# Unsplit weights for the first two subs, fp16 pairs in the second product, and an order by due times, in a chunked delta-rule attention with a gated product

## The chip, the cores and the metric

One core of a Trainium2 chip. The metric is the device time of one launch in microseconds.

## The reference, cut to what matters

A delta-rule recurrence over 768 steps for 4 x 8 heads of 48 features, then a gated product over its 3072 x 384 outputs. All inputs are float32 but the three weights, which are 64-bit floats.

```
for t in range(S):                       # q, k_n, v: [4, 8, 768, 48]
    y[:, :, t] = einsum('bhd,bhde->bhe', q[:, :, t], state)
    v_old = einsum('bhde,bhd->bhe', state, kt)
    state = state + bt * einsum('bhd,bhe->bhde', kt, vt - v_old)
x = y.transpose(0, 2, 1, 3).reshape(3072, 384)
out = ((x @ w_a) * (x @ w_b)) @ w_out    # w_a, w_b: 384 x 1536, w_out: 1536 x 384
```

## The kernel before

The 768 steps are cut into 24 chunks of 32, and two chunks (256 tokens over the batch) are a sub: 12 subs. The hidden dimension of 1536 is cut into 12 blocks of 128 (`NFC`). One block for one sub is called a unit here; there are 144.

Attention works in groups of chunks (`GROUPS`): two, five times four, two. `prep(g)` takes key norms and the key-key and key-query products of each chunk on TensorE (32 small matmuls, fp32, 64 columns wide) and, for the group, one power-of-two scale from a norm of queries and values. `solve(g)` inverts the 32 x 32 triangles of a group on VectorE, row by row; its instructions cover four chunks, and for the first group half of them is padding. `HALVES` has the first group's triangles solved in halves of 16, which small matmuls join (`wp`, `xp`). `steps(g)` goes through the chunks one after another: copy of the state (`sh`), state read `ks`, solve product `up`, output product `yp` (two groups of 32 small matmuls), state update into `S_ps`, then the scaled copy `y32`, a transpose, and the output as an fp16 high and low half (`xt`).

The gated product of a unit (`moe`): 18 matmuls of the first product, fp16, 256 columns wide (two factors, three slices of the model dimension, high x high, high x low and low x high). ScalarE copies one factor out (`a`), VectorE multiplies (`g`), ScalarE and VectorE make a high and a low half in fp32r (`ghl`). Two units later (`LAG`) `moe_out` does the second product: 6 matmuls, 384 wide, with `wo` in the same form, accumulated in two banks over the blocks of the sub.

A weight block arrives as 64-bit floats (1.15 MB). `weights` (line 550) builds the float32 bits with three integer operations on VectorE, takes the norm of the block (square on ScalarE, a matmul with ones), scales by a power of two, and splits it into halves in `wh` and `wo`; for the first four blocks (`LOWS`) the low halves come from fp32 matmuls with scaled identities. Since only three blocks have room while they arrive, the first two subs are done in pieces of two to four blocks, with partial sums in `acc`.

All operations are first written into a list (`Plan`), and `order` (line 391) sets the order on all engines: it simulates the engines with priced durations, forward and backward, six times over. `pack` keeps TensorE's small matmuls apart with a store of instruction words, and while TensorE has nothing in the first 80 us of the plan, `issue` (line 430) puts in filler matmuls of fp32 ones, 256 columns wide. Each engine, and SyncE's DMA issues, then run strictly in the written order. In the profile all planned operations have line 439, fillers line 430. An fp32 matmul shows as two records.

Of the kernel before, what the change touches and what calls it, by code (L numbers as in the profile page):

```python
# [28 lines left out]
GROUPS = [[0, 1]] + [list(range(i, i + 4)) for i in range(2, 22, 4)] + [[22, 23]]  # L29
# [3 lines left out]
HALVES = [1, 0, 0, 0, 0, 0, 0]  # L33

PARTS = [[i] for i in range(12)]
BOOST = {"first": 9e4, "prep0": 9e4, "solve0": 9e4, "steps0": 9e4, "w0": 7e4, "prep1": 5e4, "solve1": 5e4, "w1": 5e4, "w2": 4e4, "steps1": 5e4, "w3": 3e4, "w4": 3e4, "w5": 3e4, "w6": 3e4, "w7": 3e4, "w8": 3e4, "w9": 3e4, "w10": 3e4, "w11": 3e4}
LOWS = 4
# [3 lines left out]
URGENCY = {"first": 5000, "prep0": 5000, "solve0": 5000, "steps0": 5000, "w0": 3000, "w1": 2500, "w": 1500, "prep1": 3000, "solve1": 3000, "steps1": 3000, "prep": 200, "solve": 600, "steps": 500, "moe": 800, "moe_pe": 300}  # L41


class Op:
    __slots__ = ("eng", "calls", "dur", "move", "rd", "wr", "deps", "pri", "at", "end", "tag", "stream", "banks", "cold", "use", "words")

    def __init__(self, eng):
        self.eng, self.calls, self.dur, self.move = eng, [], 0.0, 0.0
        self.cold, self.use, self.words = 0.0, 0.0, 0
        self.rd, self.wr, self.deps, self.tag, self.banks = {}, {}, set(), "", set()  # L50


class Plan:
# [6 lines left out]
    def __init__(self, nc):  # L60
# [3 lines left out]
        self.stream = "first"  # L64
        self.masks = {}
# [115 lines left out]
    def add(self, eng, fn, name, args, kw):  # L181
# [5 lines left out]
        else:  # L187
            op = Op(eng)
            kind = self.stream + ("_pe" if self.stream == "moe" and eng == "PE" else "")
            op.pri = len(self.ops) - URGENCY.get(kind, URGENCY.get(kind.rstrip("0123456789"), 0))  # L190
# [12 lines left out]
        else:  # L203
            dur = self.price(eng, name, outs, ins, kw)
            op.dur += dur
            if eng == "PE":
                op.use += dur
                op.words += 4 if ins[0].dtype == F32 else 2
                if min(ins[0].shape[0], ins[0].shape[-1]) <= 64:
                    if len(op.calls) == 1:  # L210
                        op.dur += self.SWITCH
# [42 lines left out]

    def pack(self, pri, back=False):
# [10 lines left out]
        words, seen = self.STORE, 0.0  # L266
# [6 lines left out]
        while len(done) < n:  # L273
# [23 lines left out]
            while can[e] and i is None:  # L297
                i = heapq.heappop(can[e])[1]
                if ops[i].words and not back:
                    words, seen = min(self.STORE, words + (t - seen) * self.FETCH), t  # L300
                    if words < ops[i].words:
# [89 lines left out]
    def order(self):  # L391
# [23 lines left out]
        for o, o.at, o.end in zip(ops, best[1], best[2]):  # L415
            pass
# [697 lines left out]
```

## Time and profile before

| | us |
|---|---|
| runs | 685.86, 689.03, 690.97 (median 689.03) |
| profiled execution, first to last instruction | 692.9 |
| TensorE busy | 655.4 |
| VectorE busy | 418.9 |
| ScalarE busy | 256.8 |

The profiled execution's time is given by its span alone; it is 0.56% over the median of the runs. Busy time of TensorE includes the fillers, and a matmul's record lasts longer than the interval to the next one, since matmuls are pipelined.

### The profile page before, as it was taken

What the parts mean: (1) busy time and instruction counts of PE and PEld (TensorE: products, weight loads), DVE (VectorE), ACT (ScalarE), POOL (GpSimd) and SP (SyncE); (2) the same over time, 40 slices, a digit from 0 to 9 for tenths busy, and PEclk for the clock granted to TensorE, in tenths of its full rate; (3) what the DMA queues carried; (4) which work ended last, traced back from release to release, by engine and by line L of the source; (5) the groups of instructions that cost most, each with busy time, mean ns of one, the idle gap of its engine ahead of it and who ended that gap; (6) DMA issues with size and microseconds to landing.
All of it is one profiled execution on the core that took longest, in us unless ns stands there. A gap on an engine that the chain in (4) does not pass through costs nothing.

```text
span 692.9 us, 28147 instructions
## 1 busy us (share of the span) xinstructions
PE 655.4 (95%) x12994; PEld 557.3 (80%) x12994; DVE 418.9 (60%) x1125; ACT 256.8 (37%) x564; POOL 21.7 (3%) x28
## 2 busy tenths in 40 slices
PE   8879977999999989999999998999999999999997
PEld 6658755888888777788888886888877888878887
DVE  6686955888999797532436953336952249732222
ACT  2252434654822344443422244422243222332322
POOL 0000000000100010110000001100000000000000
PEclk9899985999999998999999998999999999999999
DMA  9522146441200031212200004000000000000000
GB/s 291 224 95 79 70 128 203 135 150 69 77 27 22 7 119 53 75 48 84 79 3 24 1 4 124 26 3 25 1 4 26 4 3 24 1 27 1 10 15 23
DMA packets 10581, 41.31 MB, mean 60 GB/s; under 512 B 1184, under 2 KB 4512, under 8 KB 7584
## 3 DMA queue, kind: packets, MB, share of 16 engines
q1 hardware_dynamic: 10464, 39.52, 17.3%
q8 instruction: 101, 1.65, 1.0%
q14 instruction: 16, 0.13, 0.1%
HBM read 34.80 MB, written 4.72 MB: 57 GB/s over the span
## 4 chain that ended last, share of the span: by engine, by line
PE 91%; issue 4%; DVE 4%; ACT 1%; DVEq 0%; ACTq 0%
PE bank L439 83%; PE bank L430 4%; PE S_ps L439 3%; DVE b L439 1%; DVE tmp L439 1%; DVE late L439 1%; ACT tt L439 0%; ACT sqf L439 0%; ACT late L439 0%; ACT u L439 0%; DVE xb L439 0%; DVE yt L439 0%; DVE f L439 0%; ACT wo L439 0%; DVE sw L439 0%
## 5 line engine op out<-in xcount | busy, mean ns | idle before, releaser
L439 PEld LDWEIGHTS <-wh 128*128 128x128 f16 x2592 | 242.8, 99 | 51.8 <-issue 21.0
L439 PE MATMUL bank<-xb,wh 128*128 128x256 f16 x1944 | 236.1, 275 | 0.0
L439 PE MATMUL bank<-wo,ghl 128*128 128x384 f32 x864 | 189.3, 353 | 0.0
L439 PEld LDWEIGHTS bank<-wo,ghl 128*128 128x128 f32 x864 | 144.5, 190 | 3.3
L439 ACT COPY a<-bank 128x256 f32<-128x256 f32 x144 | 53.5, 373 | 237.1 <-PE bank L439 236.8
L439 DVE TENSOR_TENSOR g<-bank,a 128x256 f32<-128x256 f32 x144 | 60.6, 421 | 126.7 <-ACT a L439 125.7
L439 DVE TENSOR_TENSOR ghl<-g,ghl 128x256 fp32r<-128x256 f32 x144 | 61.7, 430 | 33.6 <-ACT ghl L439 33.0
L439 PE MATMUL bank<-late,wh 128*128 128x256 f16 x648 | 80.2, 278 | 0.9 <-ACT late L439 0.4
L439 ACT CAST ghl<-g 128x256 fp32r<-128x256 f32 x144 | 58.1, 404 | 55.0 <-DVE g L439 54.4
L439 DVE TENSOR_TENSOR b<-b,tmp 128x60 f32<-128x60 f32 (+19 forms) x201 | 67.6, 336 | 4.4
L439 DVE TENSOR_TENSOR tmp<-b,b 128x60 f32<-128x60 f32 (+19 forms) x201 | 67.4, 335 | 4.5
L430 PE MATMUL bank<-ones 128*128 128x256 f32 x166 | 46.2, 427 | 3.3 <-DVE ones L439 3.3
L439 PEld LDWEIGHTS bank<-sh,rawb 48*32 48x32 f32 x2432 | 30.4, 110 | 16.0 <-issue 12.6
L439 PE MATMUL bank<-sh,rawb 48*32 48x48 f32 x2432 | 36.5, 209 | 6.4 <-issue 6.3
L430 PEld LDWEIGHTS bank<-ones 128*128 128x128 f32 x166 | 33.6, 212 | 8.7 <-DVE ones L439 3.2
L439 DVE STREAM_TRANSPOSE yt<-y 128x384 f32<-128x384 f32 x24 | 13.9, 577 | 33.5 <-ACT y L439 33.5
L439 PEld LDWEIGHTS bank<-f,tt 32*32 32x32 f32 x1472 | 19.5, 113 | 12.1 <-issue 7.7
L439 PE MATMUL bank<-u,at 32*32 32x48 f32 x1536 | 23.2, 206 | 5.5 <-issue 5.5
L439 PE MATMUL bank<-f,tt 32*32 32x48 f32 x1472 | 23.2, 214 | 5.1 <-issue 5.1
L439 PE MATMUL bank<-rawb 48*32 48x64 f32 x1280 | 22.6, 223 | 4.5 <-issue 4.5
L439 PEld LDWEIGHTS bank<-rawb 48*32 48x32 f32 x1280 | 19.9, 111 | 8.1 <-issue 7.8
L439 PEld LDWEIGHTS bank<-u,at 32*32 32x32 f32 x1536 | 19.1, 107 | 8.1 <-issue 6.2
(95 smaller groups left out, 490.3 us busy)
## 6 DMA issues: line engine op xcount, KB each, us to landing
rawb<-in_kqt SPq DMA_DIRECT2D x10, 896.0 KB, 6.0
late<-in_w SPq DMA_DIRECT2D x7, 1152.0 KB, 5.1
wh<-in_w SPq DMA_DIRECT2D x5, 1152.0 KB, 9.0
vnb<-in_vn SPq DMA_DIRECT2D x12, 384.0 KB, 3.2
out<-late SPq DMA_DIRECT2D x24, 192.0 KB, 1.9
knb<-in_kn SPq DMA_DIRECT2D x10, 384.0 KB, 3.4
late<-in_kqt SPq DMA_DIRECT2D x2, 896.0 KB, 5.9
late<-in_kn SPq DMA_DIRECT2D x2, 384.0 KB, 3.2
```

Source lines behind the costliest of these rows:

```text
L430: self.nc.tensor.matmul(self.pool[-1][:, 0:256], self.idle, self.idle.unsqueeze(1).broadcast_to([P, 2, P]), start=True, stop=True, skip_gr ...
L439: fn(*(self.place(a, lease) for a in args), **{k: self.place(a, lease) for k, a in kw.items()})
```

## The change

All groups have four chunks, the first ones too. The first two subs (`FULL`) use the float32 weights as `decode` makes them, with no norm and no split, in fp32 matmuls, and their outputs stay float32; block after block, without partial sums. The decoded blocks lie in one tile `wt`; when the second sub is through with a block, `split` writes the halves of the next one over it. `scales` takes the norms of all blocks for each factor, with the squares in bf16 as stationary operand and a column of ones. The second product's halves are fp16 instead of fp32r, with power-of-two scales for each factor and block (`gs`), for each chunk and batch (`n4`, from four squares and a matmul with `sel`), and for all of `w_out` (`big`). The order comes from one forward pass: each TensorE operation carries a due time, written by `slot` and `when`, the others take the latest time from what follows them. `stall` prices TensorE's instruction store in blocks of 256 words, and `pack` takes another ready operation where it would halt for over 250 ns. Key-query groups of the second group on, and the third and fourth chunk's joins, stand behind chunk 1's output product (`hold`). Fillers are 512 columns wide and end at 60 us of the plan.

```diff
-GROUPS = [[0, 1]] + [list(range(i, i + 4)) for i in range(2, 22, 4)] + [[22, 23]]
+GROUPS = [list(range(i, i + 4)) for i in range(0, NCH, 4)]
...
-EARLY = [(0, "k"), (0, "r"), (0, "b"), (2, "k"), (4, "k"), (2, "r"), (4, "r"), (0, "v"), (0, "w"), (1, "w"), (2, "v"), (4, "v"), (2, "w")]
+HALVES = [1, 0, 0, 0, 0, 0]
...
+FULL = 2
...
+LEADS = 4.0
+BASE, FRESH, UNIT = 46e3, 4.6e3, 3.75e3
+
+
+def when(v):
+    n = NFC * FULL
+    return BASE + (v * FRESH if v < n else n * FRESH + (v - n) * UNIT)
+
+
+def finish(c):
+    return 6 * c - 6 - (-2.5 if c == 4 else min(LEADS, 0.5 * max(0, c - 5)))
+
+
+def slot(c, piece):
+    if c < 2:
+        v = {
+            0: {"W": -10, "X": -9, "U": -8, "S": -7, "Q": -4, "A": -3.9},
+            1: {"W": -6.9, "K": -6, "X": -5.9, "U": -5, "Q": -4.5, "A": -4, "S": 0.2},
+        }[c].get(piece, -30)
+    elif c < 4:
+        v = (c - 2) * 5 + {"W": 0.5, "X": 1, "K": 1.5, "U": 2.5, "S": 3.5, "Q": 4, "A": 4.5}.get(piece, -30)
+    elif piece == "G":
+        v = 0.3 + 1.2 * (c - 4) if c < 8 else 18.5 + 1.2 * (c - 8) if c < 12 else finish(c - 6) - 0.5
+    else:
+        v = finish(c) - {"W": 7, "X": 6.5, "K": 5.5, "U": 4.5, "S": 3.5, "Q": 2.5, "A": 1.5}[piece]
+    return when(v)
...
+EARLY = [(0, "k"), (2, "k"), (0, "r"), (2, "r"), (0, "b"), (0, "v"), (0, "w"), (2, "v"), (1, "w"), (2, "w")]
...
+    def stall(self, o, t, pos, edge, come):
+
+        halt, each = 0.0, o.dur / o.words
+        end = pos + o.words
+        while end > edge:
+            enter = t + halt + (edge - pos) * each
+            if come > enter:
+                halt, enter = halt + come - enter, come
+            else:
+                enter = max(t, enter - self.AHEAD * each, come)
+            edge, come = edge + self.BLOCK, enter + self.FETCH
+        return halt, end, edge, come
...
+                if e == "PE" and not back and can[e] and self.stall(ops[i], t, pos, edge, come)[0] > self.STALL:
+                    other = [x for x in heapq.nsmallest(12, can[e]) if not ops[x[1]].banks - set(held)]
+                    other = [x for x in other if self.stall(ops[x[1]], t, pos, edge, come)[0] < 50.0]
+                    if other:
+                        can[e].remove(other[0])
+                        can[e].append((pri[i], i))
+                        heapq.heapify(can[e])
+                        i = other[0][1]
...
-    FETCH = 0.064
-    IDLE, SINCE, UNTIL = 440.0, 1500.0, 80e3
-    STORE = 512.0
-    SWITCH = 180.0
+    BLOCK, EDGE, FETCH, AHEAD, STALL = 256, 193, 3500.0, 30, 250.0
+    IDLE, SINCE, UNTIL = 870.0, 1500.0, 60e3
+    SWITCH = 108.0
...
-    PASSES = 6
...
+        pri = [0.0] * len(ops)
+        for i in range(len(ops) - 1, -1, -1):
+            o = ops[i]
+            late = [pri[k] - ops[k].dur - gap for k, gap in self.succ[i]]
+            pri[i] = min(late + [o.due] * (o.eng == "PE" or not late))
+            if o.stream == "load":
+                pri[i] = i - 1e9
+        for i, o in enumerate(ops):
+            if o.banks and o.eng != "PE":
+                pri[i] = min([pri[i]] + [pri[k] + self.SOON for k in o.deps if ops[k].eng == "PE"])
+        at, stop, done, total, (self.bind, self.fill) = self.pack(pri)
...
-    ghr = ring(cst, "ghl", LAG + 1, [P, 2, 256], F32R)
+    ghr = ring(cst, "ghl", LAG + 1, [P, 2, 256], F16)
...
+    WD = 6 * P + DM
+    wt = one("wt", [P, (NFC + 1) * WD], I32)
+    late = one("late", [P, 2816], I32)
+    stage = one("stage", [P, 4 * WD], I32)
...
+    slots = [late[:, 0 : 2 * WD]] + [stage[:, i * 2 * WD : (i + 1) * 2 * WD] for i in range(2)]
...
+    def decode(b):
+        load(b, "w")
+        st, d = slots[b % 3].rearrange("p (a l) -> p l a", l=2), wt[:, plain(b) : plain(b) + WD]
+        lo, hi = st[:, 0], st[:, 1]
+        V.tensor_scalar(d, hi, 5, 2, op0=ALU.logical_shift_left, op1=ALU.logical_shift_right)
+        V.scalar_tensor_tensor(d, hi, -0x40000000, d, op0=ALU.bitwise_and, op1=ALU.bitwise_or)
+        V.scalar_tensor_tensor(d, lo, 29, d, op0=ALU.logical_shift_right, op1=ALU.bitwise_or)
+        whole.add(b)
+        yield
+
...
+    def scales():
+        for b in range(NFC):
+            v = wf[:, plain(b) : plain(b) + 6 * P]
+            sq = sqr()
+            plan.due = when(b + 2.5)
+            A.activation(sq, v, AF.Square)
+            t = att()
+            with plan.group():
+                for m in range(2):
+                    for j in range(3):
+                        o = (3 * m + j) * P
+                        T.matmul(
+                            t[:, m : m + 1],
+                            sq[:, o : o + P],
+                            one16[:, 0:1],
+                            start=(m == j == 0),
+                            stop=(j == 2),
+                            skip_group_check=True,
+                        )
+            A.copy(norm[:, 2 * b : 2 * b + 2], t[:, 0:2])
...
+    def split():
+        for b in range(NFC):
+            v = wf[:, plain(b) : plain(b) + WD]
...
+            for m in range(2):
+                r, z = slice(3 * m * P, 3 * (m + 1) * P), zw[:, 2 * b + m : 2 * b + m + 1]
+                A.activation(h[:, 0, r], v[:, r], AF.Copy, scale=z)
+                V.scalar_tensor_tensor(h[:, 1, r], v[:, r], z, h[:, 0, r], op0=ALU.mult, op1=ALU.subtract)
+            e = eo[:, b : b + 1]
+            A.activation(o[:, 0], v[:, 6 * P :], AF.Copy, scale=e)
+            V.scalar_tensor_tensor(o[:, 1], v[:, 6 * P :], e, o[:, 0], op0=ALU.mult, op1=ALU.subtract)
...
+            if c // 2 < FULL:
+                if c % 2 == 0:
+                    xsub[c // 2] = xts[c // 2 % 4].rearrange("p (c j n) -> p c j n", c=2, j=3)
+                A.copy(yo, yi)
+                V.transpose(xsub[c // 2][:, c % 2].rearrange("p j n -> p (j n)"), y32)
+                yield
+                continue
...
+            for b in range(4):
+                A.activation(sqy, yb[:, b], AF.Square, accum_out=n[:, b : b + 1])
+            T.matmul(yp[:, 384:388], sel[:, 0:P], n, start=True, stop=True, skip_group_check=True)
+            V.tensor_scalar_max(t4, yp[:, 384:388], 2.0**-100)
+            root(e, t4)
+            flip(z, e, 13)
+            V.tensor_mul(yo, yi, z.unsqueeze(2).unsqueeze(3).broadcast_to([P, 4, 3, 32]))
+            V.tensor_mul(t4, e, sel[:, P : P + 4])
+            V.tensor_reduce(n[:, 0:1], t4, AX.X, ALU.add)
+            V.tensor_scalar(fact[:, c : c + 1], n[:, 0:1], n[:, 0:1], big[:, 3:4], op0=ALU.mult, op1=ALU.mult)
...
+                plan.due = when(NFC * s + fc + 0.33 * m)
+                if s < FULL:
+                    with plan.group():
+                        for j in range(3):
+                            o = plain(fc) + (m * 3 + j) * P
+                            T.matmul(
+                                ab[:, m, :].rearrange("p (c n) -> p c n", c=2),
+                                wf[:, o : o + P],
+                                xt[:, :, j, :],
+                                start=(j == 0),
+                                stop=(j == 2),
+                            )
+                    continue
...
-            A.copy(asb, ab[:, 0, :])
+            if s < FULL:
+                A.copy(asb, ab[:, 0, :])
+            else:
+                A.activation(asb, ab[:, 0, :], AF.Copy, scale=gs[:, fc : fc + 1])
             g32 = gr()
             V.tensor_mul(g32, ab[:, 1, :], asb)
-            ghl = ghr()
-            A.copy(ghl[:, 0], g32)
-            V.tensor_sub(ghl[:, 1], g32, ghl[:, 0].bitcast(F32))
+            if s < FULL:
+                ghl = g32
+            else:
+                ghl = ghr()
+                A.copy(ghl[:, 0], g32)
+                V.tensor_sub(ghl[:, 1], g32, ghl[:, 0])
...
+            plan.due = when(NFC * s + fc + LAG + 0.6 + 0.2 * i)
+            r = slice(i * P, (i + 1) * P)
+            if s < FULL:
+                o = plain(fc) + 6 * P
+                T.matmul(ops[s][i], ghl[:, r], wf[:, o : o + DM], start=first, stop=last)
...
-                part = acc[c] if s < 2 else None
-                final = fc == NFC - 1
-                ob = obs[c % 2] if final else part
-                if part is not None and c in started:
-                    V.scalar_tensor_tensor(ob, ops[s][i], facs[c], part, op0=ALU.mult, op1=ALU.add)
+                if s < FULL:
+                    A.copy(obs[i], ops[s][i])
                 else:
-                    A.activation(ob, ops[s][i], AF.Copy, scale=facs[c])
-                    started.add(c)
-                if final:
-                    SP.dma_start(out[c], ob)
-
-    started = set()
+                    A.activation(obs[i], ops[s][i], AF.Copy, scale=fact[:, c : c + 1])
+                SP.dma_start(out[c], obs[i])
...
+    queue.extend((s, list(range(NFC))) for s in range(2))
+    for b in range(3, NFC):
+        run_all(ws[b])
+        next(moes)
+        next(rest, None)
+    run_all(rest)
+    load(0, "m")
+    run_all(sc)
+    merge((moes, 8), (pr[1], 6))
+    merge((moes, 7), (sv[1], 8))
+    while pend:
+        moe_out(*pend.pop(0))
+    run_all(sp)
+    for g in range(1, NG):
```

## Rows read from the trace of the kernel before

**Rows 1.** The page: busy time, GB/s in 40 slices, two costly groups.

```profile
PE 655.4 (95%) x12994; PEld 557.3 (80%) x12994; DVE 418.9 (60%) x1125; ACT 256.8 (37%) x564; POOL 21.7 (3%) x28
...
GB/s 291 224 95 79 70 128 203 135 150 69 77 27 22 7 119 53 75 48 84 79 3 24 1 4 124 26 3 25 1 4 26 4 3 24 1 27 1 10 15 23
...
L439 PEld LDWEIGHTS bank<-wo,ghl 128*128 128x128 f32 x864 | 144.5, 190 | 3.3
...
L439 DVE STREAM_TRANSPOSE yt<-y 128x384 f32<-128x384 f32 x24 | 13.9, 577 | 33.5 <-ACT y L439 33.5
```

**Rows 2.** Stages: length, PE, PEld, DVE, ACT, POOL busy (instructions), clock, DMA.

```profile
46.00:122.00 76.00, 64.95 (x1388) 49.49 (x1388) 55.00 (x148) 29.41 (x56) 0.95 (x1) 0.83 0.34 110
122.00:259.00 137.00, 131.92 (x2508) 116.30 (x2509) 120.30 (x317) 64.71 (x141) 7.85 (x9) 1.00 0.23 75
259.00:433.00 174.00, 167.62 (x3757) 142.07 (x3749) 90.55 (x250) 66.47 (x149) 9.03 (x10) 0.96 0.17 51
```

**Rows 3.** Stages of TensorE's instructions that read the filler's ones.

```profile
0.00:122.00 122.00, 49.28 (x186) 0.86 0.46 155
```

**Rows 4.** Stages of TensorE's instructions that read the sub's input.

```profile
0.00:122.00 122.00, 4.43 (x36) 0.86 0.46 155
```

**Rows 5.** Timeline of TensorE late, product alone: start, length, instructions, count.

```profile
643.37 1.30 PE L439 MATMUL bank<-wo,ghl 128*128 128x384 f32 x6
644.52 2.14 PE L439 MATMUL bank<-xb,wh 128*128 128x256 f16 x18
646.41 1.30 PE L439 MATMUL bank<-wo,ghl 128*128 128x384 f32 x6
```

**Rows 6.** Timeline of TensorE where attention stands between products, two stretches.

```profile
363.79 1.30 PE L439 MATMUL bank<-wo,ghl 128*128 128x384 f32 x6
365.03 1.10 PE L439 MATMUL bank<-rawb 48*32 48x64 f32 x64
366.06 2.14 PE L439 MATMUL bank<-xb,wh 128*128 128x256 f16 x18
...
543.14 0.89 PE L439 MATMUL bank<-sh,rawb 48*32 48x48 f32 x64
...
544.77 1.16 PE L439 MATMUL bank<-xb,wh 128*128 128x256 f16 x9
```

**Rows 7.** TensorE's waits from 122 to 689.3 us: total, times, longest.

```profile
PE bank L439 <- issue: 11.2, 11, 2.6
```

**Rows 8.** Timeline of VectorE in the head.

```profile
27.35 1.01 DVE L439 STREAM_TRANSPOSE xn<-b 128x512 f32<-128x512 f32 x1
```

**Rows 9.** Timeline of TensorE in the head; brackets: idle before it.

```profile
30.88 0.74 PE L439 MATMUL bank<-b,tt 32*32 32x16 f32 x64
...
39.14 0.89 PE L439 MATMUL bank<-sh,rawb 48*32 48x48 f32 x64
...
47.78 1.35 PE L439 MATMUL bank<-f,tt 32*32 32x48 f32 x57 [2.11 <-issue]
...
58.22 0.88 PE L439 MATMUL bank<-u,at 32*32 32x48 f32 x64
...
61.68 2.13 PE L439 MATMUL bank<-xb,wh 128*128 128x256 f16 x18
```

**Rows 10.** The same timeline: fillers alone.

```profile
63.64 10.09 PE L430 MATMUL bank<-ones 128*128 128x256 f32 x46
```

**Rows 11.** What reads or writes the weight tile: durations min/median/max in ns.

```profile
L439 PEld LDWEIGHTS <-wh x2592: 95/98/181, 61.5 to 685.8; 128*128 128x128 f16 x200
L439 PE MATMUL bank<-xb,wh x1944: 269/273/421, 61.7 to 649.4; 128*128 128x256 f16 x195
...
L439 DVE SCALAR_TENSOR_TENSOR late<-wh,late x10: 1343/1352/1361, 69.5 to 125.9; 128x1152 int32<-128x1152 int32 x10
L439 PE MATMUL bank<-wh,neg x8: 323/326/527, 53.8 to 118.8; 128*128 128x384 f16 x8
...
DMA to landing us min/median/max: 5.4/9.0/18.7
```

More of the change, by code (lines that the diff above doesn't have):

```diff
@@ L39 @@
+EARLY = [(0, "k"), (2, "k"), (0, "r"), (2, "r"), (0, "b"), (0, "v"), (0, "w"), (2, "v"), (1, "w"), (2, "w")]
 LAG = 2
 LEAD = 4
[L41 removed]
 class Op:
[L45 removed]
+    __slots__ = ("eng", "calls", "dur", "move", "rd", "wr", "deps", "pri", "at", "end", "tag", "stream", "banks", "cold", "use", "words", "small", "due")
@@ L356, in pack @@
                 took = o.dur
-            free[e] = end = stop[i] = t + took
+            free[e] = end = stop[i] = t + took + (halt if e == "PE" and not back else 0.0)
             for b in () if back else o.banks:
@@ L564, in weights @@
             yield
+        plan.due = when(15)
         t = att()
-        with plan.group():
-            for i in range(len(part)):
-                T.matmul(t[:, 0:1], ones, sw[:, i : i + 1], start=(i == 0), stop=(i == len(part) - 1))
-        ew, zw, eo = sw[:, 4:5], sw[:, 5:6], sw[:, 6:7]
-        root(ew, t[:, 0:1])
-        V.tensor_scalar(zw.bitcast(I32), ew.bitcast(I32), -1.0, float((254 + 14) << 23), op0=ALU.mult, op1=ALU.add)
-        V.tensor_scalar(eo, ew, ew, 2.0**-28, op0=ALU.mult, op1=ALU.mult)
@@ L573, in weights @@
[L573 to L595 removed]
+        T.matmul(t[:, 0 : 2 * NFC], ones, norm, start=True, stop=True)
@@ L623, in heads @@
                 yield q, h4, 2 * q + h4 // 2, slice(q * D, q * D + D)
-    acc = [one(f"acc{i}", [P, DM]) for i in range(4)]
     loaded, whole = set(), set()
@@ L813, in steps @@
+    def steps(g, chs):
+        for c in chs:
             first, last = c == 0, c == NCH - 1
             rw, k2, vt = raw(c), knc(c), vnc(c)
+            if HALVES[g]:
+                join(g, c)
             if first:
@@ L849, in steps @@
             yp = att()
-            with plan.group():
-                if not first:
+            if not first:
+                plan.due = slot(c, "Q")
+                with plan.group():
                     for q, h4, a, cols in heads():
@@ L860, in steps @@
                         )
+            plan.due = slot(c, "A")
+            with plan.group():
                 for q, h4, a, cols in heads():
@@ L1006, in tile_kernel @@
     moes = lab("moe", moe_stream())
-    ws = [lab(f"w{i}", weights(i)) for i in range(len(PARTS))]
+    ws = [lab(f"w{b}", decode(b)) for b in range(NFC)]
+    sc = lab("scale", scales())
+    sp = lab("split", split())
     pr = [lab(f"prep{g}", prep(g)) for g in range(NG)]
     sv = [lab(f"solve{g}", solve(g)) for g in range(NG)]
-    st = [lab(f"steps{g}", steps(g)) for g in range(NG)]
+    st = [lab(f"steps{g}", steps(g, GROUPS[g] if g else [0, 1])) for g in range(NG)]
+    rest = lab("rest", steps(0, GROUPS[0][2:]))
     plan.stream = "load"
```

335 lines of the change are left out of this document (142 added, 193 removed).

## The prediction

> **What bounds the kernel now.** I read the page's first part, then stages cut where TensorE's load changes, then what TensorE does in each. TensorE is busy 95% of the span, VectorE 60%, ScalarE 37% [rows 1], so TensorE's queue sets the end. But busy is not useful: up to 122 us, 49.28 us are 186 filler records on a spare bank [rows 2, 3]. Of the gated product, only 36 first-product matmuls, two units of 144, start by then [rows 4]. (A unit is one 128-column block of the hidden layer for one 256-token sub: 18 matmuls of the first product, 6 of the second.) From 122 to 689.3 us TensorE is full. So there is a head of 122 us that does little but attention and weight preparation, a full stretch of 567 us, and 3.6 us of last eviction and store.
>
> The price of a unit comes from a stretch where nothing else runs: second products start at 643.37 and 646.41, so 3.04 us a unit, 1.15 of it from the second product's start to the next first product at 644.52, 1.89 for the 18 [rows 5]. Of the full stretch, 142 units x 3.04 = 432 us. An attention group (64 recorded small matmuls, 32 calls) costs TensorE 1.63/2 = 0.82 us where two stand side by side. The key-query group takes 1.03 us, and 1.12 with its entry: the second product ahead of it started at 363.79 and would have ended 1.15 later, at 364.94, and the next product starts at 366.06 [rows 6]. So entering costs 0.1, and a plain group alone 0.92. Some 111 groups fall in the full stretch, 106 us at 0.95; small norms are 3. Together 541, so 26 of the 567 us are waits and slow clock. Waits for "issue" are 11.2 of it [rows 7]; the granted clock of 0.96 in 259 to 433 us [rows 2] adds about 174 x 0.04 = 7.
>
> **The change part by part.** *Start.* Now the first product of block 0 must wait for norm, scaling and split of its weights and for chunk 1's output as halves; it starts at 61.68 [rows 9] and goes on steadily only from 122 us. After the change it needs, of the weights, only the three decoding operations, two of 1.35 us [rows 11] and a shorter one, 3.5 us of VectorE. I hide them under the first solve's chain; if that cover fails, 3.5 us come on top. So chunk 1's output sets the start. The first solve ends with the transpose at 27.35, at 28.4 us [rows 8]. It takes four chunks instead of two; its operations keep their shape, since the unused half was padding, but one more reduction (0.95 us) and two chunks' multiplies (1.0 each) stand ahead of it, 3 us, part of them in VectorE's waits. The two added chunks' loads stand ahead of beta, which the decay needs; their 1.3 MB at the 291 GB/s of the first slice [rows 1] are 4 us more, beside the same waits. From the first triangular join (30.88) to the end of chunk 1's state read (39.14 + 0.89) took 9.2 us [rows 9]. Behind it stand a solve and an output product of 0.88 each, four elementwise steps of 0.5 to 0.6 (the transpose 577 ns [rows 1]) and six hand-offs of about 0.2: 5.2 us. Now the same steps last until 61, since the solve product waits for its join and halts on issue for 2.11 us at 47.78, and the output product comes at 58.22 behind splits and state reads [rows 9]. So the stream starts at 28.4 + 0.3 + 9.2 + 5.2 = 43, and with one or two such halts or part of the 3 to 4 us, at 46. Bounds 42 (a shorter chain without the group norms) and 54 (all of the 7 us, two halts). Fillers run only ahead of this point; their new form costs nothing.
>
> *First two subs.* Unsplit fp32 is 6 + 2 matmuls for 18 + 6. A filler has the shape of such a first-product matmul: 46 records in 10.09 us, two a matmul, 0.44 us [rows 10]. By columns the 384-wide one is 0.66. A unit is 6 x 0.44 + 2 x 0.66 = 3.96 us, 0.92 dearer; 24 of them 95 us.
>
> *Second product in scaled fp16 pairs.* An fp16 matmul of 384 columns lasts 326 ns by the median, one of 256 lasts 273 [rows 11]; these 53 ns more than a pace of 109 (18 in 1.89 us and the hand-over) make 162, against some 180 now (1.08 us for six, hand-over taken off). Weight loads show why: 190 ns in the present form [rows 1], 98 in fp16 [rows 11], and only the second fits under 162. A unit becomes 18 x 0.109 + 6 x 0.162 = 2.94, and 120 units 353 us. Ends: 352, and 365 if the pace stays. The scale by a pointer operand lengthens ScalarE's copy by some 0.1 us, off the path.
>
> *Attention still to run after the start.* Chunks 2 to 23: 88 groups at 0.9, 21 state updates at 1.0, 20 key-query groups at 1.12, four joins at 0.9: 126 us. Each chunk's own scale replaces the group's: four squares, one small matmul, some ten VectorE operations. On TensorE that is 20 x 0.26 = 5 us (two records of 0.11 to 0.13). The rest delays an output by some 4 us, hidden by the lead of one and a half to four units that the due times give; without it each of ten subs would wait up to 4 us. The weight norms become 72 bf16 matmuls one column wide. No row has one; between 2 us (0.03, the pace of the small ones) and 8 (0.11, the fp32 norm), I take 5, since the full-width load is nearer to the second but overlaps. What goes from TensorE, splits and norms, lay in the head and counts nothing.
>
> *VectorE and queues.* VectorE is 55.0 of 76 and 120.3 of 137 us busy in the stages with decoding and the second solve [rows 2]. Up to the end of the second sub it has, after 28 us: twelve decodes 42 us, a full solve 24, preparation 10, chunks 1 to 5 12, products 10, scales 3, first splits 6: 107 in about 144. Twelve splits now go through VectorE (12 x 1.8 us) instead of eight, each between a block's last unsplit use and its first use as halves. SyncE's weight loads wait for buffers with chunk loads between them. I price these waits at nothing; the second rival is the price if that is wrong.
>
> *Idle left.* Attention is spread group by group by due time, and the order prices a store that refills in blocks; groups side by side are where the queue halts now. Of 26 us I keep about half, 14; ends 6 and 31 (5% of 584).
>
> **Sum.** Work 95 + 353 + 126 + 10 = 584; start 46, idle 14, end 3.6: 648 us of span against 692.9. The profiled run is 0.56% over the median of 689.03, so 648 x 0.9945 = **644 us**.
>
> **The rivals.** *The halts stay.* 46 + 584 + 31 + 3.6 = 665 of span, 661 us. For it: they fall inside single groups too, as at 47.78 [rows 9]. Against it: the pure stretches, with few instructions a microsecond, have none. The Trainium skill's page "Runtime: NRT & Kernel Launch", section "Instruction fetch mechanics", speaks for this rival: instructions stream in blocks of 256 and crossing into the next is "mostly hidden", so pricing blocks could win nothing. The trace here differs in that TensorE lost 11.2 us to 11 such waits, the longest 2.6, after the head [rows 7]; by the page the time would be 661, by these rows 644.
>
> *The weight stream paces the start: slower.* Twelve blocks go through three buffers, each held for a landing (9.0 us median into such a buffer [rows 11]), a wait for VectorE and 3.5 us of decoding. TensorE asks for a block each 5.2 us in the first sub (3.96 and the attention beside it), so a buffer may be held 15.6 us. If decoding queues behind the second solve and it is held 30 us, a block takes 10: 12 x 4.8 = 58 us, 706 of span, 702 us. It decides from 27 us held, where the gain is gone. Against it: VectorE's 72% in 46 to 122 us [rows 2] and the 107 in 144.
>
> *It doesn't start early.* Chunk 1's output comes at 61 us as now, and the second sub waits for chunks 2 and 3 and for blocks: some 45 us lost, no change, 685 to 692 us.
>
> *Nearly all goes.* Start 42, idle 6, the cheaper ends of the small items (577): 629 of span, 625 us.
>
> **How the numbers follow.** The forecast's own spread, 632 to 656 us, gets 0.60; halts stay (656 to 675) 0.15; nearly all goes (618 to 632) 0.15; no change 0.05; slower 0.05. The likeliest gives 644. The range 624 to 671 leaves out the two last and the far ends of the two before, two in ten. A change under 1% cannot be told from none in this kernel. Faster 0.90, same 0.05, slower 0.05.
>
> **What would show it.** In the changed profile: first products from about 46 us without filler after them; pure units of 2.94 us late; fresh units near 4 us; the second sub's end near 170 us; issue waits under half. Wrong if TensorE idles for weight blocks or for outputs of chunks 4 and 5, if a fresh unit costs over 4.5 us, or if issue waits grow.

## The result, and the profile after

The changed kernel takes **657.4 us** (median of four runs, 657.2 to 662.9) against 690.0 for the kernel before on the same chip (four runs, 685.9 to 693.7): ratio 0.959, interval 0.953 to 0.966. It is faster, as forecast, and inside the range, but the gain is 33 us where 46 were forecast. The profiled run has a span of 655.2 us; the sum said 648. So 7 of the 13 us are in the span. The other 6 are in the step from span to median: the profiled run's span lay 0.56% above the median before, and lies 0.34% below it now.

The page of the changed kernel, to be held against [rows 1] (the fourth line is the queue that brings the program itself, in packets of 16 KB):

```profile
PE 628.8 (96%) x12968; PEld 485.5 (74%) x12968; DVE 399.3 (61%) x1085; ACT 253.9 (39%) x655; POOL 22.5 (3%) x29
...
PEclk9965899999999999999999999999999999999999
...
GB/s 290 256 179 292 74 220 130 57 28 1 28 84 51 27 60 27 72 39 76 59 3 51 82 29 50 59 4 51 3 4 27 3 26 3 3 28 2 22 5 24
...
q8 instruction: 101, 1.65, 1.0%
```

TensorE is as busy as before (96%), and its weight loads are 72 us less. The stages of [rows 2]:

```profile
46.00:122.00 76.00, 65.66 (x1353) 51.10 (x1350) 39.49 (x57) 26.12 (x67) 0.00 (x0) 0.83 0.54 183
122.00:259.00 137.00, 134.56 (x2835) 104.50 (x2834) 113.75 (x321) 64.10 (x159) 10.75 (x12) 1.00 0.12 36
259.00:433.00 174.00, 172.87 (x4000) 135.92 (x3998) 114.50 (x349) 69.48 (x188) 8.84 (x10) 1.00 0.17 49
```

Behind 122 us the stream is nearly closed: 2.4 us idle in the second stage where it was 5.1, 1.1 in the third where it was 6.4, and the clock of the third is whole (0.96 before). What TensorE waited for from 122 us on, beside [rows 7]:

```profile
PE bank L484 <- issue: 2.8, 3, 1.7
PE S_ps L484 <- issue: 0.7, 1, 0.7
```

Late in the kernel, where the product stands alone, a unit is 630.90 − 627.96 = 2.94 us (3.04 in [rows 5]):

```profile
627.96 1.14 PE L484 MATMUL bank<-wt,ghl 128*128 128x384 f16 x6
628.93 2.13 PE L484 MATMUL bank<-stage,wt 128*128 128x256 f16 x18
630.90 1.14 PE L484 MATMUL bank<-wt,ghl 128*128 128x384 f16 x6
```

A unit on the unsplit weights takes 2.68 us for the first product (102.93 to 105.61) and 1.38 for the second (106.59 to 107.97), 4.06 in all; an attention group and a weight norm stand between:

```profile
102.93 2.75 PE L484 MATMUL bank<-xb,wt 128*128 128x256 f32 x12
105.61 0.88 PE L484 MATMUL bank<-f,tt 32*32 32x48 f32 x64
106.43 0.30 PE L484 MATMUL bank<-one,sqw 128*128 128x1 bf16 x6
106.59 1.54 PE L484 MATMUL bank<-wt,g 128*128 128x384 f32 x4
107.97 2.75 PE L484 MATMUL bank<-xb,wt 128*128 128x256 f32 x12
```

The head is where the forecast missed. VectorE, beside [rows 8]: the decay waits 4.86 us for beta, the first solve's transpose stands at 31.36 (27.35 before), and chunk 1's output is transposed at 55.65:

```profile
14.66 0.19 DVE L484 TENSOR_TENSOR dc<-s,bt 128x32 f32<-128x32 f32 x1 [4.86 <-DMA bt<-in_beta]
...
31.36 1.01 DVE L484 STREAM_TRANSPOSE xn<-b 128x512 f32<-128x512 f32 x1
...
55.65 0.58 DVE L484 STREAM_TRANSPOSE xb<-y 128x384 f32<-128x384 f32 x1 [2.38 <-ACT y L484]
```

TensorE in the same time, beside [rows 9]; the first product comes at 67.49:

```profile
35.59 0.32 PE L484 MATMUL bank<-b,tt 32*32 32x16 f32 x16 [1.15 <-issue]
35.77 0.88 PE L484 MATMUL bank<-vnb,tt 32*32 32x48 f32 x64
36.58 1.11 PE L484 MATMUL bank<-b,mk 128*128 128x256 f32 x2
37.62 0.59 PE L484 MATMUL bank<-wr,xn 32*16 32x16 f32 x46
39.14 0.36 PE L484 MATMUL bank<-wr,xn 32*16 32x16 f32 x18 [0.93 <-issue]
...
42.69 0.68 PE L484 MATMUL bank<-u,at 32*32 32x48 f32 x19 [0.63 <-issue]
...
49.16 0.86 PE L484 MATMUL bank<-sh,rawb 48*32 48x48 f32 x31 [3.08 <-issue]
...
54.08 1.01 PE L484 MATMUL bank<-u,at 32*32 32x48 f32 x37 [1.19 <-issue]
...
61.37 0.82 PE L484 MATMUL bank<-b,tt 32*32 32x16 f32 x43 [4.14 <-issue]
...
63.27 0.74 PE L484 MATMUL bank<-wr,xn 32*16 32x16 f32 x64
...
66.20 1.17 PE L484 MATMUL bank<-sh,rawb 48*32 48x48 f32 x45 [1.57 <-issue]
...
67.49 2.91 PE L484 MATMUL bank<-xb,wt 128*128 128x256 f32 x6
```

Two things are to be read here. First, add up the matmuls from one halt to the next: 16 + 64 + 2 + 46 = 128 from 35.59 to 39.14, each with its weight load: 256 instructions. From each halt to the next, up to the one at 66.20, it is 128 again (127 in one case). The page fits this: 12,968 matmuls and as many weight loads are 101.3 times 256, and the queue of the program brought 101 packets. So I read these halts as waits for the next block of the program. Second, behind chunk 1's output (56.2 us) the first product could run; between them stand chunk 2's joins and state read, with halts of 4.14 and 1.57 us. The halts from 28 to 68 us sum to 12.7 us (7 of them). The granted clock is at half, 1.2 GHz, for most of the time from 37 to 71 us (the digits 6, 5 on the PEclk line); it fell while TensorE did small attention matmuls between these waits.

### The profile page after: what moved, and what is told of

The parts are those of the page before. It is cut to its first block, busy times and chain, and to the rows that moved or that the text cites. A ratio compares the mean times of both kernels' runs of the same rounds, so it can differ in the third digit from the quotient of the medians.

```text
span 655.2 us, 28091 instructions
## 1 busy us (share of the span) xinstructions
PE 628.8 (96%) x12968; PEld 485.5 (74%) x12968; DVE 399.3 (61%) x1085; ACT 253.9 (39%) x655; POOL 22.5 (3%) x29
## 4 chain that ended last, share of the span: by engine, by line
PE 90%; DVE 4%; DMA 3%; issue 2%; SPq 0%; ACT 0%
PE bank L484 87%; PE S_ps L484 3%; DMA rawb<-in_kqt 2%; DVE wt L484 2%; DMA stage<-in_w 1%; DVE b L484 1%; DVE tmp L484 1%; SPq L484 0%; DVE xn L484 0%; ACT ob L484 0%; DVE vnb L484 0%; ACT tt L484 0%; DVE at L484 0%; ACT norm L484 0%; DVE dt L484 0%
## 5 line engine op out<-in xcount | busy, mean ns | idle before, releaser
L484 PE MATMUL bank<-xb,wt 128*128 128x256 f16 (+1 forms) x1800 | 251.1, 292 | 0.5 <-issue 0.5
L484 PEld LDWEIGHTS <-wt 128*128 128x128 f16 x2160 | 208.7, 98 | 36.0 <-issue 0.9
L484 PE MATMUL bank<-wt,ghl 128*128 128x384 f16 x720 | 137.1, 327 | 0.0
L484 ACT ACTIVATE a<-bank,gs 128x256 f32<-128x256 f32 x120 | 56.8, 474 | 177.4 <-PE bank L484 177.2
L484 PEld LDWEIGHTS <-ghl 128*128 128x128 f16 x720 | 65.7, 98 | 36.4
L484 PE MATMUL bank<-stage,wt 128*128 128x256 f16 x648 | 77.5, 273 | 0.0
L484 DVE TENSOR_TENSOR ghl<-g,ghl 128x256 f16<-128x256 f32 x120 | 52.1, 435 | 32.1 <-ACT ghl L484 31.2
L484 ACT CAST ghl<-g 128x256 f16<-128x256 f32 x120 | 48.5, 404 | 43.3 <-DVE g L484 42.9
L484 PEld LDWEIGHTS bank<-xb,wt 128*128 128x128 f32 x288 | 55.0, 195 | 10.8
L484 DVE TENSOR_TENSOR b<-b,tmp 128x31 f32<-128x31 f32 (+20 forms) x170 | 57.2, 337 | 4.1
L484 DVE TENSOR_TENSOR tmp<-b,b 128x31 f32<-128x31 f32 (+20 forms) x170 | 57.0, 336 | 4.2
L484 PEld LDWEIGHTS bank<-sh,rawb 48*32 48x32 f32 x2432 | 30.4, 111 | 14.6 <-issue 11.2
```

What stands on the lines that cost most here:

```text
L484: fn(*(self.place(a, lease) for a in args), **{k: self.place(a, lease) for k, a in kw.items()})
```

## The experiments

Theory A after the result: the start is late because blocks of the program arrive slowly beside the weight loads, because chunk 2's groups stand ahead of the first product, and because the solve ends 4 us later; each of these taken away should be worth its price. Theory B: something else is as late as the start, and gives the gain back. Twelve kernels were run, on three chips (e1 to e4, e5 to e8, e9 to e12); the kernel before took 692.3, 684.9 and 686.3 us there. The changed kernel was not run on the last two chips, so spans are compared first, and ratios to the kernel before where a time counts. The four spans of the changed kernel lie between 655.2 and 661.0 us, and those of e5_hold between 653.5 and 659.7: a difference of 1 or 2 us between two profiled runs shows nothing.

**e1_first: chunk 2's joins and state read behind the first product.** The changed line stands at both joins (`W` and `X`), the added one at the state read (`K`).

```diff
-        plan.behind = set(hold if c > 1 else ())
+        plan.behind = set(hold + [opened[0] + 1] if c > 1 else ())
...
+                plan.behind = set([opened[0] + 1] if c == 2 else ())
```

> The changed kernel, with the joins and the state read of chunk 2 ordered behind the first unit's first product; all else as it was. Theory A (supply): TensorE's queue gets at most a block of 256 instructions each 3.5 us, every halt of the changed kernel falls at one position modulo 256, and the small matmuls put ahead of the first product use up two blocks there; with the product first, it starts near 57 us instead of 67.5, the two halts of 4.1 and 1.6 us shrink because an fp32 unit takes few instructions, and the time falls by 4 to 8 us, to about 651. Theory B (clock): the half clock from 37 to 71 us sets the start; the first unit then runs at half clock, the order changes nothing in sum, and the time stays within 2 us of 657.4.

656.2 us (656.1 to 659.8), ratio 0.951 (0.947 to 0.955), span 654.1. The first product came at 66.68 only: its solve ended 2 us later, and chunk 2's other state read, which was not held, went ahead at 60.75 and halted 2.52 us. The start near 57 us and the 651 us of Theory A did not come; the time is Theory B's. As far as this edit reached, the order alone is worth nothing that stands clear of the spread.

**e2_quiet: the weight loads of blocks 3 to 5 wait for chunk 1's output** (one column of each buffer is written from it).

```diff
                 V.transpose(xsub[c // 2][:, c % 2].rearrange("p j n -> p (j n)"), y32)
+                if c == 1:
+                    for st_ in slots:
+                        V.tensor_copy(st_[:, 0:1], y32.bitcast(I32)[:, 0:1])
```

> The changed kernel, with a one-column write from chunk 1's output into each of the three weight buffers, so that blocks 3 to 5 are loaded only after it. Theory A2 (contention): a block of instructions takes 3.55 us while no weight load runs and 4.8 to 7.3 us while one does, since both come by DMA; without loads in 41 to 56 us, the halts at 45.8 and 52.6 us (3.1 and 1.2 us) fall under 1 us each and chunk 1's output stands 3 to 5 us sooner, near 52 us. Rival: instructions come at a fixed pace whatever else is loaded, and the output stays within 1 us of 56.2. The whole time can go either way, since blocks 3 to 5 come later: 650 to 665.

Halts from 28 to 68 us fell from 12.7 to 4.6, the longest from 4.1 to 1.2, and the first product came at 57.07, 10.4 us sooner. But the sign that was named, chunk 1's output near 52 us, did not come:

```profile
56.18 0.57 DVE L484 STREAM_TRANSPOSE xb<-y 128x384 f32<-128x384 f32 x1
```

The output is there at 56.75, as late as in the changed kernel (56.23), which was the rival's number. Its chain of joins began 2.5 us later (34.06 for 31.58), behind a later solve and more fillers, and its five halts were 4.6 us for 7.0: the loads do stretch the blocks, but only by some 2 us here. The first product is sooner because this order puts chunk 2's groups behind it. And the time is 659.2 (658.8 to 661.8), ratio 0.953 (0.950 to 0.957), span 659.8: nothing gained. Theory B had to be taken seriously: where did 10 us go?

**e3_blind: the order written with the delivery of program blocks priced at nothing.**

```diff
-    BLOCK, EDGE, FETCH, AHEAD, STALL = 256, 193, 3500.0, 30, 250.0
+    BLOCK, EDGE, FETCH, AHEAD, STALL = 256, 193, 0.0, 30, 250.0
```

> The changed kernel, with the delivery time of an instruction block priced at zero when the order is made, so that nothing is moved out of the way of a halt. If the pricing is what emptied the full stretch (my step on idle time): issue waits after 122 us, 4 us in all now, come back to 10 to 20 us, and the time rises by 8 to 20 us, to 665 to 677. If the due times alone spread attention enough, as the page on instruction fetch would have it that crossings are mostly hidden: waits stay under 7 us after 122 us, and the time is within 4 us of 657.4.

667.5 us (666.9 to 669.4), ratio 0.966 (0.963 to 0.970), span 665.4: 10 us of span. The waits from 122 us on:

```profile
PE bank L484 <- issue: 7.2, 7, 1.5
PE S_ps L484 <- issue: 1.6, 2, 0.9
```

8.8 us where the changed kernel has 3.5, and the granted clock in 175 to 200 us is 0.73, which costs 25 x 0.27 = 7 more. Spreading small groups by blocks is worth about what the prediction's "idle left" gave it: 10 us here, 26 less 14 there.

**e4_beta: beta loaded ahead of the r rows** (one run).

```diff
-EARLY = [(0, "k"), (2, "k"), (0, "r"), (2, "r"), (0, "b"), ...
+EARLY = [(0, "k"), (2, "k"), (0, "b"), (0, "r"), (2, "r"), ...
```

> The changed kernel, with beta and the masks loaded ahead of the two chunk pairs' key and query rows. My prediction has beta's place as one cost of the later solve: VectorE then no longer waits 4.9 us for it, and the first solve's last transpose starts at 27.5 to 28.5 us instead of 31.4. Rival: the second pair's rows, landing at 14.4 us, and the halt of 2.2 us behind them set the solve; beta's place is worth under 1 us, and the transpose starts at 30.5 to 31.5 us.

657.2 us, span 655.2 as before the edit. The decay is ready at 10.0 us instead of 14.66, but the solve's transpose stands at 31.23 instead of 31.36: the second pair's rows, and a halt of 2.95 us in the key-query groups, are as late. The beta wait in the rows above ends last on paper; without it the solve ends 0.13 us sooner.

**e5_hold: as e1_first, with chunk 2's output product against the state (`Q`) held too.**

```diff
+                plan.behind = set([opened[0] + 1] if c == 2 else ())
                 plan.due = slot(c, "Q")
```

> As e1_first, with the output matmuls of chunk 2 against the state (the group that went ahead of the first product in e1_first and halted 2.52 us there) held behind unit 0's first product too. Theory A (what stands in the way of the first product is chunk 2's groups, each crossing a block border at half clock): with all of them behind, the product of unit 0 starts at 60 to 62 us against 67.49, right behind chunk 1's transposed output, and the time falls by 4 to 6 us against the changed kernel's 657.4, to 651 to 653. Theory B (those groups have to run anyway, and each border costs its halt wherever it falls; the first product only changes places with them): first product at 60 to 62 too, and the time within 2 us of 657.4.

First product at 61.66, span 653.5, 659.1 us (655.5 to 661.8), ratio 0.962 (0.956 to 0.968). Of 5.8 us of earlier start 1.7 are left in the profiled span, and nothing that is clear of the spread of the runs. The first second product comes 2.8 us sooner (75.6 for 78.4): the other 3 us are chunk 2's groups, which only changed places with it. Theory B. The start could have come sooner still: chunk 1's output is there at 57.0, and six filler records stand between it and the first product, from 57.42 to 61.66.

**e6_both: e5_hold and e2_quiet in one** (the edits of both).

> e5_hold and e2_quiet in one: chunk 2 behind the first product, and the weight loads of blocks 3 to 5 held back until chunk 1's output is transposed, so that the program's blocks arrive every 4 us in the head. Theory A: first product at 54 to 57 us; the gain of the order (4 to 6 us) is kept, the loss of e2_quiet (later waits for weight blocks, 1.7 us) too: 652 to 656. Theory B (the stream of weight tiles is what the first two thirds of the fresh units wait for, so anything that delays it comes back one to one): as e2_quiet, 658 to 662, with TensorE's idle time between 60 and 110 us longer by what the start gained.

First product at 55.06, 12.4 us sooner, halts in the head 2.9 us; 659.8 us (657.4 to 660.2), ratio 0.964 (0.958 to 0.969), span 655.4: again nothing. In the head the blocks now come 3.55 to 4.0 us apart. The first and the last of five halts (timeline of TensorE), and chunk 1's output, 1.5 us sooner than in the changed kernel (timeline of VectorE):

```profile
37.73 0.40 PE L484 MATMUL bank<-b,tt 32*32 32x16 f32 x14 [1.09 <-issue]
...
52.56 0.86 PE L484 MATMUL bank<-u,at 32*32 32x48 f32 x31 [0.31 <-issue]
...
54.18 0.57 DVE L484 STREAM_TRANSPOSE xb<-y 128x384 f32<-128x384 f32 x1
```

The time is what Theory B said, but not for its reason: TensorE has no wait between 60 and 122 us. This time the trace names the place. Timelines of TensorE, of ScalarE and of SyncE's queue, and the page's clock line:

```profile
165.88 1.50 PE L484 MATMUL bank<-f,tt 32*32 32x48 f32 x64 [4.61 <-ACT tt L484]
...
123.41 0.61 ACT L484 ACTIVATE sqf<-wt,po 128x384 f32<-128x384 f32 x1
...
124.15 0.84 ACT L484 ACTIVATE sqf<-knb 128x768 f32<-128x768 f32 x1
...
165.20 1.17 ACT L484 COPY tt<-b 128x256 f32<-128x256 f32 x2 [7.40 <-DVE b L484]
...
101.96 0.33 SPq L484 DMA_DIRECT2D knb<-in_kn  x1
...
PEclk9867999999779999999999999999999999999999
```

TensorE runs out of work and waits 4.6 us for the second group's solved blocks, ready at 165 us; in the changed kernel they were ready at the same time,

```profile
165.22 2.27 ACT L484 COPY tt<-b 128x256 f32<-128x256 f32 x4 [1.49 <-DVE b L484]
```

and TensorE, being later, never waited. The granted clock is at half twice (the two 7s): right behind this wait, and again from about 181 us, behind an issue wait of 1.64 us. Its mean is 0.94 in 122 to 175 us and 0.96 in 175 to 259: 53 x 0.06 = 3.2 and 84 x 0.04 = 3.4, together 6.5 us. With 1.2 us more of issue waits in these stages, 4.6 + 6.5 + 1.2 = 12.3 us are given back. That is at least what the start gained: of its 12.4 us some 3 are chunk 2's groups changing places, as in e5_hold (the first second product comes 9.5 us sooner, 68.9 for 78.4). e2_quiet has the same wait, 4.6 us, and the same two 7s. And the rows say why the solve is late: its first step, the squares of the k rows, stands on ScalarE at 124.15 right behind the last square of the weights, though the rows' load was issued at 101.96. Both write one buffer, so the program's order binds them.

**e7_whole: the first solve in one piece of 32, no joins.**

```diff
-HALVES = [1, 0, 0, 0, 0, 0]
+HALVES = [0, 0, 0, 0, 0, 0]
```

> The first group's triangular solve in one piece of 32 rows instead of two of 16: VectorE's substitution has 31 steps instead of 15, and the joins of chunks 0 to 3 (33 matmuls each, 132 with their weight loads 264 instructions, one whole block of the program) are gone. Theory A (TensorE's instruction count sets the head: a block costs 3.6 to 7 us there): the longer solve (some 8 to 12 us more on VectorE, the two sizes' work being 15 and 31 steps of up to twice the width) is paid back by half only: first product at 68 to 72, time 657 to 664. Theory B (VectorE's chain of decode and solve sets the head, and TensorE's halts lie beside it): all of the longer solve shows: first product at 75 to 80, time 665 to 672.

The solve ends at 48.5 instead of 32.4, 16 us later and more than either theory said; the first product comes at 75.65, 8.2 us later, so the joins that went paid half of it back. They are more than the expectation counted: 520 recorded matmuls, with their weight loads 1040 instructions, or four blocks (the queue of the program has 97 packets for 101). By the numbers, start and time are Theory B's; that half of the longer solve does not show is Theory A's. 667.1 us (666.0 to 668.0), ratio 0.974 (0.969 to 0.979), span 664.2. The span is 9 us longer, about what the start lost: with nothing won at the start, nothing was given back.

**e8_early: as e2_quiet, released at chunk 0's output.**

```diff
-                if c == 1:
+                if c == 0:
```

> As e2_quiet, but the weight loads of blocks 3 to 5 are released at chunk 0's transposed output (about 44 us) instead of chunk 1's (56 us). Theory A (loads that run beside the program's own fetches stretch each block from 3.6 to 5 to 7 us): the blocks up to 44 us come 3.6 to 4 us apart as in e2_quiet, those behind it 5 to 7 apart; first product at 61 to 64, and the later waits for weight blocks are mostly gone: 652 to 656. Theory B (the head's gain is given back because the same loads still have to run beside some fetch): first product at 62 to 66, time 656 to 659.

First product at 62.80, 659.7 us (658.5 to 663.1), ratio 0.964 (0.959 to 0.970), span 657.0. The halts beside the released loads are back in part (2.38 us ahead of 57.38; 6.7 us from 28 to 68), and TensorE waits 1.9 us for the second solve, ready at 168. Start and time are Theory B's (the time 0.7 us over its bound).

**e9_swap: e6_both with the second group's row norms ahead of the squares of the weights.**

```diff
-    run_all(sc)
     merge((moes, 8), (pr[1], 6))
+    run_all(sc)
```

> e6_both with one exchange: the second group's row norms (squares on ScalarE, sums on VectorE) come ahead of the squares of the weights instead of behind their last twelve. Theory A (the head's 12 us were lost again because TensorE then ran out of work at 161 us and waited 4.6 us for the second group's solved blocks, which ended at 165 us in that kernel and in the changed one alike, with the clock at half behind it): the solve ends at 153 to 158 us, that wait is gone and the clock stays whole there; span 655.4 less 6 to 10, that is 645 to 649, ratio 0.945 to 0.955 by the runs of before on the same chip. Theory B (another chain, the weights' scales and splits, is as late as the solve): the wait moves to a bank fed by the split weights, span 653 to 658, no change.

**649.5 us** (649.3 to 649.7), ratio 0.948 (0.941 to 0.956), span 647.6. ScalarE copies the second group's solved blocks from 140 to 148, where that began at 165, and the clock line has no gap any more:

```profile
147.98 0.64 ACT L484 COPY tt<-b 128x256 f32<-128x256 f32 x1
...
PEclk9776999999999999999999999999999999999999
```

From 122 to 259 us the view of TensorE's waits has no row at all. The start is 10.9 us sooner than in the changed kernel and the span 7.6 us shorter; 2.4 us of halts between 60 and 122 us are part of the rest. Theory A's 645 to 649 of span holds, in all four runs (647.3 to 647.6; e6_both 655.4 to 658.2). Against e6_both 4.6 us of waiting, 6.5 of half clock and 3.6 of issue waits are gone, and the later start (1.5) and those halts (2.4) are new: 10.8 us, where the medians of the spans differ by 10.2. The planner writes the whole order anew for each edit, so other things moved as well (the order of weight loads among them).

**e10_swap_hold: e5_hold with the same exchange.**

> e5_hold (chunk 2 behind the first product, weight loads as in the changed kernel) with the same exchange. There TensorE waited only 1.6 us for VectorE and ScalarE between 122 and 259 us, so theory A gives 1 to 3 us less than its span of 653.5, that is 650.5 to 652.5; the solve ends 5 to 10 us sooner with nobody waiting for it. Theory B: as e5_hold within 1 us.

656.9 us (655.3 to 660.5), ratio 0.960 (0.953 to 0.967), span 655.0, 1.5 over e5_hold, which is within the spread: nothing gained. The last solved block is copied at 154, but with the loads back in the head the blocks are late again:

```profile
46.03 0.69 PE L484 MATMUL bank<-u,at 32*32 32x48 f32 x19 [2.83 <-issue]
...
53.05 0.69 PE L484 MATMUL bank<-sh,rawb 48*32 48x48 f32 x19 [3.95 <-issue]
```

Halts are 8.5 us from 28 to 68 (5.3 in e5_hold) and another 3.8 from 68 to 122 (1.8 there). In these runs the exchange gains only together with the quiet head: the two bounds seem to lie within a few us of each other, so that one taken away shows the other.

**e11_one: only sub 0 on the unsplit weights.**

```diff
-FULL = 2
+FULL = 1
...
-    queue.extend((s, list(range(NFC))) for s in range(2))
+    queue.append((0, list(range(NFC))))
```

(with the scales worked out earlier and the rest of the steps in the order that this needs)

> Only the first 256 rows use the weights unsplit; rows 256 to 511 use the fp16 halves, whose scales and splits so have to be there twelve units sooner. Theory A (TensorE's time by units decides from 122 us on): twelve units at 2.94 us in place of 4.06, 13 us less than the changed kernel: span 640 to 644. Theory B (the second group of units is what covers the scales and splits on VectorE and ScalarE; without it TensorE waits for them): the 13 us come back as waits between 100 and 175 us, and the clock falls behind them: span 655 to 670.

668.1 us (666.5 to 671.5), ratio 0.976 (0.969 to 0.983), span 664.4. Twelve units are 1.12 us cheaper each, and TensorE waits for the split weights:

```profile
PE bank L484 <- DVE wt L484: 14.9, 2, 12.7
```

between 122 and 259 us, with a clock of 0.84 in 122 to 175. The dearer units of sub 1 are what hides scales and splits.

**e12_half2: the kernel before with only its second product in fp16 pairs** (fixed powers of two as scales).

```diff
-    wo = one("wo", [P, NFC, 2, DM], F32R)
+    wo = one("wo", [P, NFC, 2, DM], F16)
```

(and the same type for the product's halves)

> The kernel before with only the second product changed to fp16 pairs (fixed powers of two as scales, so no scales to work out); first product of all units on the split weights as before, order and groups as before. The prediction's price: a unit of 3.04 us becomes 2.94, over 144 units 14 us, of which those beside waits in the first 122 us (some 20 units) show nothing: 12 to 14 us less than before, ratio 0.980 to 0.983. Rival (the weight loads of the second product were hidden beside the matmuls, so that only the matmuls' own 2.07 us count): within 3 us of before, ratio over 0.995.

673.7 us (673.1 to 674.6) against 686.3, ratio 0.984 (0.977 to 0.990): 12.6 us. The unit is 2.94 us here too:

```profile
626.82 1.14 PE L439 MATMUL bank<-wo,ghl 128*128 128x384 f16 x6
627.80 2.13 PE L439 MATMUL bank<-xb,wh 128*128 128x256 f16 x18
629.76 1.14 PE L439 MATMUL bank<-wo,ghl 128*128 128x384 f16 x6
```

So of the 33 us some 13 come from the second product. The other 20, by difference and so not shown by a run of their own, are what the earlier start and the closer order bring beyond the price of the 24 dearer units.

## Why the prediction was right, and where a size was off

**The mechanism held, the number in part by luck.** The 657 us lie just outside the forecast's own spread of 632 to 656, in the band that was given to "the halts stay", whose mechanism did not come: the start was 21 us late, and the terms behind it were 14 us too high. Of the signs that were named, pure units of 2.94 us, fresh units near 4 and issue waits under half came; a start near 46 and an end of the second sub near 170 us did not (67.5, and about 202). The head of fillers is gone, first products start ahead of split weights, and TensorE works through to the fp16 units. The unit prices held: 2.94 as forecast, confirmed by itself in e12_half2; 4.06 for 3.96 on the unsplit weights, 2.4 us over 24 units.

**The step that was mis-sized is the start: "So the stream starts at 28.4 + 0.3 + 9.2 + 5.2 = 43, and with one or two such halts or part of the 3 to 4 us, at 46".** It was 67.5, outside its bounds of 42 to 54. By its own terms: the solve ended at 32.4, +4.0, all of the "3 to 4 us" and not a part (by e4_beta it is the second pair's rows and not beta); from there chunk 1's output took 23.8 us (to 56.2) for 14.7, +9.1, with five halts of 7.0 us in sum, not one or two, and at half clock; and 11.3 us stood between that output and the first product, other groups and two halts of 5.7 us, which the step had at zero. 28.4 + 14.7 + 4.0 + 9.1 + 11.3 = 67.5. The rows of before had shown the halt of 2.11 us; that this chain crosses a border every 128 recorded matmuls, and runs at half clock (1.50 us a group where 0.88 is the full-clock time), was left out. The loads beside it are the smaller part: the four blocks from the first halt to the fifth take 18.5 us in the changed kernel and 14.8 with the loads held back (e6_both), and there the chain from the solve's end to chunk 1's output still takes 21.3 us for 14.7.

**Other terms made up most of it.** Behind the start the sum had 602 us, and 588 were needed. Idle was 14 in the sum; it was 3.5 us of issue waits and about 2 of half clock. Weight norms (5 in the sum) took about 2: six of them pass in 0.16 us (106.43 to 106.59). Part of chunk 2's attention was done ahead of the start, some 3 us. Less the 2.4 us of dearer units, this is about 12 of the 14; the rest is not assigned.

**The step "I price these waits at nothing" was right by accident.** VectorE's second solve was ready at 165 us, in time for a stream that began at 67. For a stream from 46 us it would have been late, as e6_both shows from 55: a wait of 4.6 us and a clock at half behind it. The forecast's 107 us of VectorE work in 144 was a sum of work, and did not look at the order in which ScalarE feeds it; what was late was one chain, squares to sums to solve, behind twelve squares of weights on another engine. So even a start near the forecast's would, by e6_both, have given a span of about 655, not 648, until the exchange in e9_swap.

**The rivals.** "The halts stay" fell: 3.5 us after the head for 11.2. The Trainium skill's page "Runtime: NRT & Kernel Launch", section "Instruction fetch mechanics", has the crossing of a block "mostly hidden"; the runs here agree behind the head of the changed kernel, where four waits stand against some 84 borders (10,758 matmuls and their loads), and differ elsewhere: e3_blind, whose order does not price the crossing, is 10 us longer, and in the head each crossing shows 0.6 to 4.1 us. "The weight stream paces the start: slower" did not come, since the fresh stream had no row of waits for weights; e11_one shows its near relative, split weights that pace sub 1, 14.9 us of waits. "It doesn't start early" and "nearly all goes" fell with the start at 67.5.

**Open.** That loads and program blocks share the DMA engines is argued from e2_quiet, e6_both and e8_early against e5_hold and e10_swap_hold, and from the DMA share: 0.95 or more from 42 to 62 us in the changed kernel, where blocks come 4.9 to 7.3 us apart, and 0.04 from 36 to 49 us in e6_both, where they come 3.55 to 3.7 apart. The delay inside a DMA engine was not seen by itself. How much of the half clock in the head is due to the halts, and how much to the shape of the matmuls, was not separated.

## What to carry to other kernels

A gain at the start of a stream is worth at most the slack of the next chain that must be ready: look up when the next group's inputs are ready in the same trace, and forecast the smaller of the two. When an edit moves a milestone by 10 us and the time by none, search the later stages for a wait that was not there, name its producer, and follow it back to what it was queued behind; the remedy here was one line on an engine that was 39% busy. In a stretch of many small matmuls, count instructions as well as microseconds.

## What the runs showed of the hardware that was not expected

TensorE's program came in blocks of 256 instructions: 128 recorded matmuls with their loads from halt to halt, and 101 packets for 101.3 blocks (97 for 97.6 in e7_whole). In the head of the changed kernel, where small matmuls pass faster than blocks come, TensorE resumed at 35.59, 39.14 and 42.69 us, 3.55 apart; beside weight loads at 49.16, 54.08, 61.37 and 66.20, 4.8 to 7.3 apart. The four blocks from the first of these halts to the fifth took 17.7 to 20.3 us where weight loads ran beside them (the changed kernel, e5_hold, e10_swap_hold), and 14.8 to 16.5 us where the loads were held back (e2_quiet, e6_both, e9_swap). Right behind a wait of 4.6 us in a full stream (e6_both) the granted clock fell to half, which cost about 3 us more; behind an issue wait of 1.64 us it fell again and cost as much, while in the changed kernel an issue wait of 1.7 us in the same stage left it whole.
